# Attention products of two heads in turn on row and column tiles of TensorE, each chain held back until its banks and operands are there

## The chip, the cores and the metric

The kernel runs on one core of a Trainium2 chip. The metric is the device time of one execution in microseconds (us), as the median of the executions shown.

## What is computed

A decaying linear attention over 4 batches, 8 heads of 48 columns and 768 steps feeds a dense layer with a gated unit (384 to 2048 to 384), and that feeds a layer of eight experts, of which each token takes one (384 to 1024 to 384). All data are float32.

```python
f = 1.0 / (1.0 + np.exp(-f_logit))
for t in range(S):
    state = f[:, :, t, :, None] * state + np.einsum('bhd,bhe->bhde', k[:, :, t], v[:, :, t])
    y[:, :, t] = np.einsum('bhd,bhde->bhe', q[:, :, t], state)
...
h = x @ w_in
relu6 = np.clip(h + 3.0, 0.0, 6.0)
g = h * relu6 / 6.0
return (g @ w_out).astype(np.float32)
...
h = np.maximum(x[mask] @ w1[e], 0.0)
ye = h @ w2[e]
out[mask] = gate_w[mask, None] * eom[mask, e, None] * ye
```

## The kernel before

The 3072 tokens are worked in eight blocks (0 to 7) of 384 (TB): each batch is two blocks, its first half and its second. A block's attention is four **units** (pr 0 to 3), each for a pair of heads; there are 32 units, and the text numbers them n = 4 * block + pr. `attention` (from L199) does one unit. In SBUF the first head of a pair lies on partitions 0 to 47, the second on 64 to 111 (R is 112). A block has three chunks (c) of 128 tokens.

In a unit VectorE and ScalarE turn the decay into running products (two scans, L224 and L226) and scale keys and queries with them (kb L231, qt L233). Then TensorE works, all in plain float32:

- pk (L239): three transposes of the keys; ScalarE copies them to kn (L241).
- pa (L246): for each chunk and head a product of 48 rows by 128 columns, into one PSUM bank for each head; VectorE masks each bank into at (L248).
- pkv (L255, L256): keys by values, for the first head on columns 0 to 63 of the array and for the second from 64 on; VectorE adds them up into the running state st (L263 to L270), and ScalarE puts its negative into sbd (L274), one of two buffers in turn.
- py (L281, L282, L284): the unit's result. The values lie in DRAM with 96 columns, in which the two heads' columns alternate in groups of 16 and the other head's are zero. So three products of 96 columns on the whole array, one with the masked scores of each head and one with the state of both, add up to a chunk (two in the first chunk of a batch).

The result is split into a high and a low float32r part: xth by ScalarE (L290), xtl by VectorE (L291). Units 0 to 2 of a block fill 96 partitions each of one third of the block's 384 columns. The fourth fills the last 32 partitions of all three thirds, with three copies and three subtractions.

`mlp` (L301) then does the block's dense layer with products in three terms (high by high, high by low, low by high): 144 "up" products into ph (L296 to L298) and 144 "down" products into acc (L309 to L311), each 128 by 128 by 384. `between` issues the units of the next block among those of the current one, so that they are there when the next block begins. `choose` and `route` (px, pl, pt, pr) pick each token's expert and scatter its row to DRAM. After block 7 come the eight experts (yacc).

PSUM has three buffers for pk, pa, pkv, py, px, pl, pt and pr together (pool ps_m, tag m). The order on each engine isn't that of the code: a scheduler sets it at build time from a model of the engines' times (schedule_with_timeline_sim, last line), within the data's dependencies. On the chip each engine works its list in that order and waits at an instruction whose operands aren't there. All loads go through SP's queue in its own list's order. Weights of the dense layer are loaded and split on VectorE during the attention of blocks 0 and 1 (split64, L128 to L146); `fill` (L470) writes 16 blocks of padding to DRAM once the last of them is issued.

Of the kernel before, what the change touches and what calls it, by code (L numbers as in the profile page):

```python
# [10 lines left out]
F32 = mybir.dt.float32  # L11
F32R = mybir.dt.float32r
# [5 lines left out]
ALU = mybir.AluOpType  # L18
# [4 lines left out]
P = 128  # L23
B, H, S, D = 4, 8, 768, 48
NT = B * S
DM = H * D
KD = DM // P
FF = 2048
NF = FF // P
# [3 lines left out]
TB = 384  # L33
# [15 lines left out]
def fused(ctx: ExitStack, tc: tile.TileContext, q, k, fl, v, vt, w_in, w_out, wg, w1, w2, out):  # L49
# [123 lines left out]
    def raw_of_block(tag):  # L173
        return blkp.tile([P, KD, TB], F32R, tag=tag, name="raw").rearrange("p k t -> p (k t)").bitcast(F32)[:, 0:SW]

# [14 lines left out]


# [5 lines left out]
    for i in range(2):  # L197
        t = at1.tile([R, NCH, 96], F32, name=f"sbd{i}")
        nc.gpsimd.memset(t, 0.0)  # L199
        sbds.append(t)  # L200
    state, ready = {}, []

    def attention(blk, pr, xth, xtl):
# [6 lines left out]
        vs = at2.tile([P, NCH, 2, 96], F32, tag="vs", name="vs")  # L210
# [30 lines left out]
        nc.scalar.copy(kn, pk)  # L241
        at = at2.tile([P, 2, NCH, CH], F32, tag="at", name="at")
        pas = [ps_m.tile([P, NCH, CH], F32, tag="m", name=f"pa{x}") for x in range(2)]
        for c in range(NCH):
            for pa, rows in zip(pas, heads):
                nc.tensor.matmul(pa[:, c, :], lhsT=kb[rows, c, :], rhs=qt[rows, c, :], start=True, stop=True)  # L246
        for x, pa in enumerate(pas):
            nc.vector.tensor_tensor(out=at[:, x], in0=pa, in1=nmask[:, None, :].to_broadcast([P, NCH, CH]),  # L248
                                    op=ALU.mult)
# [3 lines left out]
        cols = lambda t, x: t.rearrange("p (j x i) -> p j x i", j=3, x=2)[:, :, x, :]  # L253
# [18 lines left out]
        for hf in range(2):  # L272
            rows = slice(64 * hf, 64 * hf + D)
            nc.scalar.mul(  # L274
                sbd[rows].rearrange("p c (j x i) -> p c j x i", j=3, x=2)[:, c0:, :, hf, :],
                st[rows, c0:, :].rearrange("p c (j i) -> p c j i", j=3), -1.0)
# [8 lines left out]
        if pr < 3:  # L285
            parts = [(slice(0, 96), slice(0, 96), pr)]
        else:
            parts = [(slice(96, 128), slice(32 * j, 32 * j + 32), j) for j in range(3)]
        for dst, src, j in parts:
            nc.scalar.copy(xth[dst, j, :], py[src])  # L290
            nc.vector.tensor_tensor(out=xtl[dst, j, :], in0=py[src], in1=xth[dst, j, :].bitcast(F32),  # L291
                                    op=ALU.subtract)
# [139 lines left out]
    SYNC = mybir.DependencyInfo(mybir.DependencyClass.Sync, mybir.DependencyReason.DATA)  # L432

# [3 lines left out]

    def after_all(ins, others):
        for o in others:
            tc.add_manual_dep(ins.ins, o.ins.name, SYNC, reason="scattered rows")  # L440

# [3 lines left out]
    def att_unit(blk, pr):  # L445
        if pr == 0:
            xts[blk] = [blkp.tile([P, KD, TB], F32R, tag=n, name=n) for n in ("xth", "xtl")]
        attention(blk, pr, *xts[blk])
# [145 lines left out]
    for blk in range(NB):  # L594
        if blk == NB - 1:
            attc.close()
            ma = second.enter_context(tc.tile_pool(name="ma", bufs=1, side="right", reuse_waits="tile"))
            rank()

            spare = cycle([partial(raw_of, work)] * 2 + [partial(raw_of_block, n) for n in ("xth", "xtl")])  # L600
# [18 lines left out]
        acc = mlp(blkp, *xts.pop(blk), *wfirst, NF, relu6, between)  # L619
# [56 lines left out]
    with tc.If(general > 0):  # L676
# [4 lines left out]
        with ExitStack() as es:  # L681
# [3 lines left out]
            zsel = gp.tile([R, 176], F32, name="zsel")  # L685
            nc.vector.memset(zsel, 0.0)
            nc.vector.memset(zsel[0:D, 80:81], 1.0)
            nc.vector.memset(zsel[64:R, 96:97], 1.0)
# [3 lines left out]
            with tc.For_i(0, B * H // 2, 1) as n:  # L692
# [6 lines left out]
                for e in range(D):  # L699
# [9 lines left out]
                    j, i = divmod(e, 16)  # L709
                    c = 80 - (32 * j + i)  # L710
# [8 lines left out]
        with ExitStack() as es:  # L719
# [5 lines left out]
            with tc.For_i(0, NB, 1) as nb:  # L725
# [4 lines left out]
                for pr in range(3):  # L730
                    nc.sync.dma_start(out=xg[0:96, pr, :],
                                      in_=yv[bass.ds(nb, 1), pr].rearrange("a p t -> p (a t)"))
                    nc.sync.dma_start(out=xg[96:P, pr, :],
                                      in_=yv[bass.ds(nb, 1), 3, 32 * pr:32 * pr + 32].rearrange("a p t -> p (a t)"))
# [48 lines left out]
def layouts(inp):  # L783
# [9 lines left out]
    v = np.asarray(inp["v"]).reshape(B * H // 2, 2, 2, NCH, CH, 3, 16).transpose(0, 2, 4, 3, 1, 5, 6)  # L793
    vp = np.zeros((B * H // 2, 2, CH, NCH, 2, 3, 2, 16), v.dtype)
    for x in range(2):
        vp[:, :, :, :, x, :, x] = v[:, :, :, :, x]
    v = vp.reshape(B * H // 2, 2, CH, NCH, 2, 96)
    vt = np.asarray(inp["v"]).reshape(B * H // 2, 2, S, D).transpose(0, 3, 1, 2)
    order = []
    for j in range(KD):  # L800
        for h0, js in ((2 * j, range(3)), (6, [j])):
            for i3 in js:
                for h in (h0, h0 + 1):
                    order += [h * D + 16 * i3 + i for i in range(16)]
# [29 lines left out]
```

## Time and profile before

| what | value |
|---|---|
| median of 3 runs | 886.04 us (884.87 to 886.79) |
| time of the profiled execution | 883.24 us |
| its span in the profile | 881.4 us |
| TensorE (PE) busy | 848.4 us, 96% of the span |
| VectorE (DVE) busy | 540.1 us, 61% |
| ScalarE (ACT) busy | 406.1 us, 46% |
| mean granted clock of TensorE | 0.972 |

A clock of 1.0 is 2.4 GHz, 0.5 is 1.2 GHz. A float32 product stands in the records as two matmuls, a float32r product as one. Starts are exact, ends of matmuls are modelled and overlap the next start; so the time that a product takes is read here from one start to the next.

### The profile page before, as it was taken

What the parts mean: (1) busy time and instruction counts of PE and PEld (TensorE: products, weight loads), DVE (VectorE), ACT (ScalarE), POOL (GpSimd) and SP (SyncE); (2) the same over time, 40 slices, a digit from 0 to 9 for tenths busy, and PEclk for the clock granted to TensorE, in tenths of its full rate; (3) what the DMA queues carried; (4) which work ended last, traced back from release to release, by engine and by line L of the source; (5) the groups of instructions that cost most, each with busy time, mean ns of one, the idle gap of its engine ahead of it and who ended that gap; (6) DMA issues with size and microseconds to landing.
All of it is one profiled execution on the core that took longest, in us unless ns stands there. A gap on an engine that the chain in (4) does not pass through costs nothing.

```text
span 881.4 us, 14159 instructions
## 1 busy us (share of the span) xinstructions
PE 848.4 (96%) x5370; PEld 788.6 (89%) x5370; DVE 540.1 (61%) x1138; ACT 406.1 (46%) x864; POOL 60.2 (7%) x103
## 2 busy tenths in 40 slices
PE   8589999999999999999999999999999999999994
PEld 4469999999999999999999998999898999999994
DVE  7999995678546579554668743446364453555441
ACT  4557574456335346533545533435354343454421
POOL 1000000100100100010010010010100011101111
PEclk8668999999999999999999999999999999999998
DMA  7554576222111022121122000014154064255510
GB/s 220 183 175 118 178 246 193 65 69 67 36 59 59 22 81 69 30 73 44 38 66 67 30 28 15 1 31 157 46 197 159 29 203 146 82 172 197 164 55 28
DMA packets 40106, 85.78 MB, mean 97 GB/s; under 512 B 5185, under 2 KB 23394, under 8 KB 40028
## 3 DMA queue, kind: packets, MB, share of 16 engines
q1 hardware_dynamic: 36748, 75.29, 27.3%
q0 software_dynamic: 3280, 9.49, 3.0%
q8 instruction: 44, 0.72, 0.3%
q14 instruction: 34, 0.28, 0.1%
HBM read 68.92 MB, written 16.26 MB: 97 GB/s over the span
## 4 chain that ended last, share of the span: by engine, by line
PE 67%; DMA 3%; DVE 2%; issue 1%; ACT 1%; SPq 0%; POOL 0%; POOLq 0%; DVEq 0%; ACTq 0%
PE ph L296 9%; PE ph L297 9%; PE ph L298 9%; PE acc L309 6%; PE acc L310 5%; PE acc L311 5%; PE yacc L297 4%; PE pa L246 4%; PE yacc L298 3%; PE yacc L296 3%; DMA raw<-in_w 2%; PE py L281 2%; PE py L284 1%; PE py L282 1%; PE py L583 1%
## 5 line engine op out<-in xcount | busy, mean ns | idle before, releaser
L297 PE MATMUL ph<-xtl,wih 128*128 128x384 f32 x384 | 132.1, 344 | 1.3 <-DVE xtl L291 1.3
L296 PE MATMUL ph<-xth,wih 128*128 128x384 f32 x384 | 131.5, 344 | 1.4 <-DVE gf L334 0.8
L309 PE MATMUL acc<-woh,gh 128*128 128x384 f32 x384 | 131.6, 344 | 0.4 <-ACT gh L335 0.4
L298 PE MATMUL ph<-xth,wil 128*128 128x384 f32 x384 | 131.6, 343 | 0.0
L310 PE MATMUL acc<-wol,gh 128*128 128x384 f32 x384 | 130.0, 339 | 0.0
L334 DVE SCALAR_TENSOR_TENSOR gf<-gf,ph 128x384 f32<-128x384 f32 x128 | 70.5, 552 | 96.4 <-ACT gf L333 95.7
L311 PE MATMUL acc<-woh,gl 128*128 128x384 f32 x384 | 124.2, 340 | 0.0
L333 ACT ACTIVATE gf<-ph,three 128x384 f32<-128x384 f32 x128 | 74.2, 581 | 102.0 <-PE ph L298 100.4
L340 DVE SCALAR_TENSOR_TENSOR hl<-ph,hh 128x256 fp32r<-128x256 f32 (+7 forms) x72 | 39.0, 543 | 88.9 <-ACT hh L339 81.4
L335 ACT CAST gh<-gf 128x384 fp32r<-128x384 f32 x128 | 65.4, 512 | 58.2 <-DVE gf L334 54.9
L339 ACT ACTIVATE hh<-ph 128x256 fp32r<-128x256 f32 (+7 forms) x72 | 34.5, 481 | 116.1 <-PE ph L298 110.9
L336 DVE TENSOR_TENSOR gl<-gf,gh 128x384 fp32r<-128x384 f32 x128 | 70.8, 554 | 27.6 <-ACT gh L335 26.9
L297 PEld LDWEIGHTS ph<-xtl,wih 128*128 128x128 f32 x384 | 73.1, 190 | 3.2 <-DVE xtl L291 2.2
L296 PEld LDWEIGHTS ph<-xth,wih 128*128 128x128 f32 x384 | 72.6, 190 | 3.3 <-DVE gf L334 1.4
L297 PE MATMUL yacc<-hl,w2h 128*128 128x256 f32 (+7 forms) x216 | 71.7, 338 | 2.5 <-DVE hl L340 2.5
L298 PEld LDWEIGHTS ph<-xth,wil 128*128 128x128 f32 x384 | 73.1, 190 | 1.2
L309 PEld LDWEIGHTS acc<-woh,gh 128*128 128x128 f32 x384 | 72.1, 188 | 1.7 <-ACT gh L335 0.7
L310 PEld LDWEIGHTS acc<-wol,gh 128*128 128x128 f32 x384 | 72.2, 188 | 1.0
L311 PEld LDWEIGHTS acc<-woh,gl 128*128 128x128 f32 x384 | 71.3, 188 | 0.8 <-DVE gl L336 0.2
L296 PE MATMUL ph<-xh,w1h 128*128 128x256 f32 (+7 forms) x216 | 71.9, 334 | 0.0
L297 PE MATMUL ph<-xl,w1h 128*128 128x256 f32 (+7 forms) x216 | 71.7, 332 | 0.0
L298 PE MATMUL ph<-xh,w1l 128*128 128x256 f32 (+7 forms) x216 | 71.5, 332 | 0.0
(159 smaller groups left out, 1593.7 us busy)
## 6 DMA issues: line engine op xcount, KB each, us to landing
raw<-in_w SPq DMA_DIRECT2D x24, 512.0 KB, 6.1
raw<-in_w SPq DMA_DIRECT2D x32, 384.0 KB, 3.6
vs<-in_v SPq DMA_DIRECT2D x32, 288.0 KB, 3.1
raw<-in_w_in SPq DMA_DIRECT2D x12, 512.0 KB, 3.9
raw<-in_w_out SPq DMA_DIRECT2D x12, 512.0 KB, 3.7
xt<-in_fl SPq DMA_DIRECT2D x32, 168.0 KB, 2.9
kt<-in_k SPq DMA_DIRECT2D x32, 168.0 KB, 2.3
qt<-in_q SPq DMA_DIRECT2D x32, 168.0 KB, 3.4
```

The source lines that it names most:

```text
L246: nc.tensor.matmul(pa[:, c, :], lhsT=kb[rows, c, :], rhs=qt[rows, c, :], start=True, stop=True)
L296: nc.tensor.matmul(ps, lhsT=wh, rhs=xh, start=first, stop=False)
L297: nc.tensor.matmul(ps, lhsT=wh, rhs=xl, start=False, stop=False)
L298: nc.tensor.matmul(ps, lhsT=wl, rhs=xh, start=False, stop=last)
L309: nc.tensor.matmul(acc[t], lhsT=gh[:, ts_], rhs=w2h[:, f, :], start=f == 0, stop=False)
L310: nc.tensor.matmul(acc[t], lhsT=gh[:, ts_], rhs=w2l[:, f, :], start=False, stop=False)
L311: nc.tensor.matmul(acc[t], lhsT=gl[:, ts_], rhs=w2h[:, f, :], start=False, stop=f == nf - 1)
L333: nc.scalar.activation(gf, ph, AF.Relu, bias=three)
L334: nc.vector.scalar_tensor_tensor(out=gf, in0=gf, scalar=6.0, in1=ph, op0=ALU.min, op1=ALU.mult)
L335: nc.scalar.copy(gh, gf)
L336: nc.vector.tensor_tensor(out=gl, in0=gf, in1=gh.bitcast(F32), op=ALU.subtract)
L340: nc.vector.scalar_tensor_tensor(out=gl, in0=ph, scalar=0.0, in1=gh.bitcast(F32), op0=ALU.max, op1=ALU.subtract).ins)
```

## The change

- pa: the products of the two heads are issued in turn (second head, first head, then the next chunk), in an order that the scheduler has to keep (`in_turn`).
- py: the values and the state of each head get 64 columns of their own (48 and 16 of zeros). Each chunk is two products for each head, one with the scores and one with the state, on 64 columns of the array: the first head's on columns 0 to 63, the second's on 64 to 127, in turn.
- pkv: the same products as before, in turn, second head first.
- The first pa product of a unit waits for kn and for the subtraction that freed the unit before's py bank (`after_all(products[0], freed)`); the first py product waits for both masks and both state copies (`after_all(products[0], masked)`).
- xth and xtl become one tile xx. A unit's copy and subtraction cover 128 partitions. The fourth unit of a block goes to a tile yx instead, and six transfers from SBUF to SBUF carry its rows to their places in xx. Rows of w_in are reordered on the host to match.
- The branch for extreme decays and loads, which these inputs don't take, follows the new layout.

```diff
@@ -238,22 +247,24 @@
         kn = at1.tile([P, NCH, R], F32, tag="kn", name="kn")
-        nc.scalar.copy(kn, pk)
+        freed[0:1] = [nc.scalar.copy(kn, pk)]
         at = at2.tile([P, 2, NCH, CH], F32, tag="at", name="at")
         pas = [ps_m.tile([P, NCH, CH], F32, tag="m", name=f"pa{x}") for x in range(2)]
-        for c in range(NCH):
-            for pa, rows in zip(pas, heads):
-                nc.tensor.matmul(pa[:, c, :], lhsT=kb[rows, c, :], rhs=qt[rows, c, :], start=True, stop=True)
+        products = [nc.tensor.matmul(pas[x][:, c, :], lhsT=kb[heads[x], c, :], rhs=qt[heads[x], c, :], start=True,
+                                     stop=True) for c in range(NCH) for x in (1, 0)]
+
+        after_all(products[0], freed)
+        in_turn(products)
+        masked = []
...
-        for c in range(NCH - half):
-            nc.tensor.matmul(pkv[0:64, c, :], lhsT=kn[:, c, 0:64], rhs=cols(vs[:, c, 0, :], 0), start=True, stop=True)
-            nc.tensor.matmul(pkv[64:R, c, :], lhsT=kn[:, c, 64:R], rhs=cols(vs[:, c, 1, :], 1), start=True, stop=True)
+        wide = (slice(0, 64), heads[1])
+        in_turn([nc.tensor.matmul(pkv[wide[x], c, :], lhsT=kn[:, c, wide[x]], rhs=vs[:, c, x, 0:D], start=True,
+                                  stop=True) for c in range(NCH - half) for x in (1, 0)])
...
-        py = ps_m.tile([96, TB], F32, tag="m", name="py")
+        for x in range(2):
+            masked.append(nc.scalar.mul(sbd[heads[x], c0:, x, 0:D], st[heads[x], c0:, :], -1.0))
+        py = ps_m.tile([P, TB], F32, tag="m", name="py")
+        products = []
         for c in range(NCH):
             cs = slice(c * CH, (c + 1) * CH)
             first = half == 0 and c == 0
-            nc.tensor.matmul(py[:, cs], lhsT=vs[:, c, 0, :], rhs=at[:, 0, c, :], start=True, stop=False)
-            nc.tensor.matmul(py[:, cs], lhsT=vs[:, c, 1, :], rhs=at[:, 1, c, :], start=False, stop=first)
+            halves = [(x, py[64 * x:64 * x + 64, cs]) for x in (1, 0)]
+            products += [nc.tensor.matmul(o, lhsT=vs[:, c, x, :], rhs=at[:, x, c, :], start=True, stop=first)
+                         for x, o in halves]
             if not first:
-                nc.tensor.matmul(py[:, cs], lhsT=sbd[:, c, :], rhs=qt[:, c, :], start=False, stop=True)
...
+                products += [nc.tensor.matmul(o, lhsT=sbd[:, c, x, :], rhs=qt[:, c, :], start=False, stop=True)
+                             for x, o in halves]
+        after_all(products[0], masked)
+        in_turn(products)
+
+        yx = xx[:, :, pr, :] if pr < 3 else at1.tile([P, 2, TB], F32R, tag="yx", name="yx")
+        nc.scalar.copy(yx[:, 0, :], py)
+        freed[1:] = [nc.vector.tensor_tensor(out=yx[:, 1, :], in0=py, in1=yx[:, 0, :].bitcast(F32), op=ALU.subtract)]
+        if pr == 3:
+            for j in range(KD):
+                for x in range(2):
+                    nc.sync.dma_start(out=xx.bitcast(F32)[64 * x + D:64 * x + 64, :, j, :],
+                                      in_=yx.bitcast(F32)[64 * x + 16 * j:64 * x + 16 * j + 16])
```

TensorE's list, first half of unit 18 (block 4), before: pa_3512 is the bank of the first head, pa_3513 that of the second.

```order
L239 MATMUL pk<-ident,kb 128x112 x2
L246 MATMUL pa_3512<-qt,kb 128x128 [waits DMAHW1_49,PE_49]
L246 MATMUL pa_3512<-qt,kb 128x128 x2
L310 MATMUL acc_3103<-wol,gh 128x384
...
L297 MATMUL ph<-xtl,wih 128x384
L246 MATMUL pa_3513<-qt,kb 128x128 [waits DVE_49]
L246 MATMUL pa_3513<-qt,kb 128x128 x2
L298 MATMUL ph<-xth,wil 128x384
...
L255 MATMUL pkv<-vs,kn 64x48 [waits DMAHW3_49,Activation_49]
```

The same place with the change:

```order
L253 MATMUL pa_3566<-qt,kb 128x128 [waits DMAHW0_49,DVE_49,Activation_49]
L253 MATMUL pa_3565<-qt,kb 128x128 [waits PE_49]
L253 MATMUL pa_3566<-qt,kb 128x128
L253 MATMUL pa_3565<-qt,kb 128x128
...
L266 MATMUL pkv<-vs,kn 48x48 [waits DMAHW4_49,PE_49]
...
L291 MATMUL py<-at,vs 64x128 [waits DVE_49,Activation_49]
L291 MATMUL py<-at,vs 64x128 x3
L294 MATMUL py<-qt,sbd_160 64x128 x2
```

Before, the two heads' pa chains stand apart, with seven products of the dense layer between them, and pkv stands five further on. Now the six pa products are one chain with the heads in turn, pkv follows at once, and 28 products of the dense layer stand between pkv and py, which is one chain too.

TensorE's list at the entrance of block 3, before: the end of unit 15's py (sbd_160), then what follows it up to the block's first up product.

```order
L284 MATMUL py<-qt,sbd_160 96x128
L246 MATMUL pa_2853<-qt,kb 128x128 [waits Activation_49]
...
L297 MATMUL ph<-xtl,wih 128x384
...
L281 MATMUL py<-at,vs 96x128 [waits DVE_49]
...
L310 MATMUL acc_2333<-wol,gh 128x384
...
L296 MATMUL ph<-xth,wih 128x384
```

The same place with the change, unit 15's py and unit 16's pa and pkv, up to block 3's first up product:

```order
L294 MATMUL py<-qt,sbd_160 64x128 x2
L248 MATMUL pk<-ident,kb 128x112 [waits PE_49]
L248 MATMUL pk<-ident,kb 128x112 x2
L253 MATMUL pa_2900<-qt,kb 128x128 [waits DMAHW2_49,DVE_49,Activation_49]
L253 MATMUL pa_2899<-qt,kb 128x128 [waits PE_49]
...
L266 MATMUL pkv<-vs,kn 48x48 [waits DMAHW4_49]
...
L310 MATMUL ph<-xx,wih 128x384 [waits DMAHW1_49,DMAHW0_49]
```

Before, 38 products of the dense layer (24 and 14) stand between unit 15's py and block 3's first up product. Now none does, and that product waits for two of the six transfers.

SP's list with the change, ahead of the six transfers of unit 7 (for block 1); the two xs_d rows are the last of the 16 fills:

```order
L479 DMA xs_d<-pad 128x3x388 [waits DMAHW0_49]
L481 DMA xs_d<-pad 128x388 [waits DMAHW1_49]
L223 DMA vs<-in_v 128x384 [waits DMAHW2_49,PE_49]
L221 DMA qt<-in_q 112x384 [waits DMAHW3_49,PE_49]
L305 DMA xx<-yx 16x2x384 [waits DMAHW4_49,DVE_49]
L305 DMA xx<-yx 16x2x384 [waits DMAHW5_49]
```

Before, block 1's tiles needed no transfer; now its six stand behind the fills.

## Rows read from the trace of the kernel before

**Rows 1.** Busy times by stretch: stretch, us, then each engine's busy us, PEclk, DMA, GB/s.

```profile
63.33:71.60 8.27, 7.44 (x24) 6.27 (x25) 8.24 (x17) 5.99 (x14) 0.00 (x0) 0.50 0.34 105
71.60:140.00 68.40, 68.40 (x453) 65.15 (x453) 64.41 (x129) 43.42 (x92) 0.00 (x0) 1.00 0.67 212
140.00:553.00 413.00, 412.51 (x2770) 386.39 (x2769) 254.80 (x586) 192.17 (x442) 20.48 (x30) 1.00 0.17 52
```

**Rows 2.** Waits of TensorE from 72 to 553 us: total, times, longest.

```profile
PE py L284 <- ACT sbd L274: 0.5, 1, 0.5
```

**Rows 3.** Groups on TensorE from 140 to 553 us: matmul records and busy us.

```profile
L246 PE MATMUL pa<-qt,kb 48*128 48x128 f32 x276 | 41.8, 291 | 0.0
```

**Rows 4.** Timeline of TensorE, one head's pa chain in unit 18: start, us, what.

```profile
472.57 0.33 PE L296 MATMUL ph<-xth,wih 128*128 128x384 f32 x1
472.75 0.34 PE L297 MATMUL ph<-xtl,wih 128*128 128x384 f32 x1
473.01 0.93 PE L246 MATMUL pa<-qt,kb 48*128 48x128 f32 x6
473.88 0.44 PE L298 MATMUL ph<-xth,wil 128*128 128x384 f32 x1
474.16 0.34 PE L296 MATMUL ph<-xth,wih 128*128 128x384 f32 x1
```

**Rows 5.** The same view, py products of unit 17.

```profile
467.10 0.38 PE L281 MATMUL py<-at,vs 128*96 128x128 f32 x2
467.32 0.38 PE L282 MATMUL py<-at,vs 128*96 128x128 f32 x2
```

**Rows 6.** The same view, unit 0, where both heads' pa stand together.

```profile
9.15 0.94 PE L246 MATMUL pa<-qt,kb 48*128 48x128 f32 x12
10.02 0.91 PE L69 MATMUL warm<-kb,pad 112*128 112x384 f32 x2
```

**Rows 7.** The same view, pkv of unit 17 (12 records from 462.61 on), and what follows.

```profile
462.61 0.26 PE L255 MATMUL pkv<-vs,kn 128*64 128x48 f32 x1
...
463.09 0.46 PE L281 MATMUL py<-at,vs 128*96 128x128 f32 x2
```

**Rows 8.** Copies and masks behind the chains: least, median and most ns.

```profile
L290 ACT CAST xth<-py x48: 457/472/493, 16.9 to 555.7; 96x384 fp32r<-96x384 f32 x24, 32x384 fp32r<-32x384 f32 x24
L291 DVE TENSOR_TENSOR xtl<-py,xth x48: 528/552/557, 17.3 to 556.3; 96x384 fp32r<-96x384 f32 x24, 32x384 fp32r<-32x384 f32 x24
L248 DVE TENSOR_TENSOR at<-pa,nmask x64: 528/557/559, 10.4 to 545.6; 128x384 f32<-128x384 f32 x64
```

**Rows 9.** SP's issues, back to back, and kt's time from issue to landing (last number, us).

```profile
0.81 0.41 SPq L212 DMA_DIRECT2D xt<-in_fl  x1
1.28 0.41 SPq L212 DMA_DIRECT2D kt<-in_k  x1
kt<-in_k SPq DMA_DIRECT2D x32, 168.0 KB, 2.3
```

**Rows 10.** SP's issues of the 16 fills, first and last, and their landing.

```profile
121.23 0.43 SPq L471 DMA_DIRECT2D xs_d<-pad  x1
...
136.96 0.88 SPq L473 DMA_DIRECT2D xs_d<-pad  x1
xs_d<-pad SPq DMA_DIRECT2D x8, 582.0 KB, 6.9
```

**Rows 11.** TensorE's clock early on: a long wait in the timeline, and stretches.

```profile
42.89 0.82 PE L239 MATMUL pk<-ident,kb 112*128 112x112 f32 x3 [3.32 <-DVE kb L231]
37.50:40.90 3.40, 1.34 (x9) 0.90 (x8) 3.33 (x9) 2.43 (x7) 0.00 (x0) 1.00 0.67 215
40.90:51.20 10.30, 8.31 (x42) 5.98 (x43) 10.09 (x23) 4.85 (x11) 0.00 (x0) 0.50 0.56 178
69.46 0.52 PE L297 MATMUL ph<-xtl,wih 128*128 128x384 f32 x1
69.78 0.52 PE L298 MATMUL ph<-xth,wil 128*128 128x384 f32 x1
```

More of the change, by code (lines that the diff above doesn't have):

```diff
@@ L189, in load_second, with after_all @@
         return [partial(first, kt) for kt in range(KD)] + [partial(second, i) for i in range(NFE // 2)]
+    SYNC = mybir.DependencyInfo(mybir.DependencyClass.Sync, mybir.DependencyReason.DATA)
+    def after_all(ins, others):
+        for o in others:
+            tc.add_manual_dep(ins.ins, o.ins.name, SYNC, reason="all of them first")
     zero = at1.tile([R, TB], F32, name="zero")
@@ L197, in fused, with in_turn, attention @@
     for i in range(2):
-        t = at1.tile([R, NCH, 96], F32, name=f"sbd{i}")
+        t = at1.tile([R, NCH, 2, 64], F32, name=f"sbd{i}")
         nc.gpsimd.memset(t, 0.0)
         sbds.append(t)
-    state, ready = {}, []
-    def attention(blk, pr, xth, xtl):
+    state, ready, freed = {}, [], []
+    ORDER = mybir.DependencyInfo(mybir.DependencyClass.NoSync, mybir.DependencyReason.DATA)
+    def in_turn(products):
+        for a, b in zip(products, products[1:]):
+            tc.add_manual_dep(b.ins, a.ins.name, ORDER, reason="one head after the other")
+    def attention(blk, pr, xx):
         b, half = divmod(blk, 2)
@@ L271, in attention @@
         c0 = 1 - half
[L272 to L276, printed above, removed]
-        py = ps_m.tile([96, TB], F32, tag="m", name="py")
+        for x in range(2):
+            masked.append(nc.scalar.mul(sbd[heads[x], c0:, x, 0:D], st[heads[x], c0:, :], -1.0))
+        py = ps_m.tile([P, TB], F32, tag="m", name="py")
+        products = []
         for c in range(NCH):
@@ L280, in attention @@
             first = half == 0 and c == 0
-            nc.tensor.matmul(py[:, cs], lhsT=vs[:, c, 0, :], rhs=at[:, 0, c, :], start=True, stop=False)
-            nc.tensor.matmul(py[:, cs], lhsT=vs[:, c, 1, :], rhs=at[:, 1, c, :], start=False, stop=first)
+            halves = [(x, py[64 * x:64 * x + 64, cs]) for x in (1, 0)]
+            products += [nc.tensor.matmul(o, lhsT=vs[:, c, x, :], rhs=at[:, x, c, :], start=True, stop=first)
+                         for x, o in halves]
             if not first:
-                nc.tensor.matmul(py[:, cs], lhsT=sbd[:, c, :], rhs=qt[:, c, :], start=False, stop=True)
[L285 to L292, printed above, removed]
+                products += [nc.tensor.matmul(o, lhsT=sbd[:, c, x, :], rhs=qt[:, c, :], start=False, stop=True)
[10 more added lines that the diff above has]
+                                      in_=yx.bitcast(F32)[64 * x + 16 * j:64 * x + 16 * j + 16])
     def mm3(ps, wh, wl, xh, xl, first, last):
@@ L436, in free_of @@
             tc.declare_no_dep(ins.ins, o.ins, reason="rows of their own")
-    def after_all(ins, others):
-        for o in others:
-            tc.add_manual_dep(ins.ins, o.ins.name, SYNC, reason="scattered rows")
     xts = {}
@@ L446, in att_unit @@
         if pr == 0:
-            xts[blk] = [blkp.tile([P, KD, TB], F32R, tag=n, name=n) for n in ("xth", "xtl")]
-        attention(blk, pr, *xts[blk])
+            xts[blk] = blkp.tile([P, 2, KD, TB], F32R, tag="xx", name="xx")
+        attention(blk, pr, xts[blk])
     wfirst = first_weights(m1)
@@ L598, in fused @@
             rank()
-            spare = cycle([partial(raw_of, work)] * 2 + [partial(raw_of_block, n) for n in ("xth", "xtl")])
+            two = blkp.tile([P, 2, KD, TB], F32R, tag="xx", name="xx").rearrange("p h k t -> p h (k t)").bitcast(F32)
+            spare = cycle([partial(raw_of, work)] * 2 + [lambda: two[:, 0, 0:SW], lambda: two[:, 1, 0:SW]])
             for part in weights(0, ma, lambda: next(spare)()):
@@ L618, in fused @@
         between(-1)
-        acc = mlp(blkp, *xts.pop(blk), *wfirst, NF, relu6, between)
+        xx = xts.pop(blk)
+        acc = mlp(blkp, xx[:, 0], xx[:, 1], *wfirst, NF, relu6, between)
         if blk == NB - 1:
@@ L708, in fused @@
                     nc.vector.tensor_tensor(out=sg, in0=sg, in1=qg, op=ALU.mult)
-                    j, i = divmod(e, 16)
-                    c = 80 - (32 * j + i)
+                    c = D - 1 - e
                     for t in range(2):
@@ L729, in fused @@
                 yv = ya_d.rearrange("h (b r) p t -> (h b) r p t", r=4)
[L730 to L734, printed above, removed]
+                for j in range(KD):
+                    for x in range(2):
+                        for dst, pr, src in ((64 * x, j, D * x), (64 * x + D, 3, D * x + 16 * j)):
+                            n = D if pr < 3 else 16
+                            nc.sync.dma_start(out=xg[dst:dst + n, j, :],
+                                              in_=yv[bass.ds(nb, 1), pr, src:src + n].rearrange("a p t -> p (a t)"))
                 split(xth, xtl, xg, nc.gpsimd)
@@ L790, in pairs @@
         return np.ascontiguousarray(o.reshape(B * H // 2, P, S)[:, :R])
[L793 to L797, printed above, removed]
+    v = np.asarray(inp["v"]).reshape(B * H // 2, 2, 2, NCH, CH, D).transpose(0, 2, 4, 3, 1, 5)
+    v = np.concatenate([v, np.zeros(v.shape[:-1] + (64 - D,), v.dtype)], -1)
     vt = np.asarray(inp["v"]).reshape(B * H // 2, 2, S, D).transpose(0, 3, 1, 2)
@@ L800, in layouts @@
     for j in range(KD):
[L801 to L804, printed above, removed]
+        for x in range(2):
+            order += [(2 * j + x) * D + i for i in range(D)] + [(6 + x) * D + 16 * j + i for i in range(16)]
     w_in = np.asarray(inp["moe_w_in"])[np.array(order)].reshape(KD, P, FF).transpose(1, 0, 2)
```

16 lines of the change are left out of this document (6 added, 10 removed).

## The prediction

> **What bounds the kernel now.** First the busy times by stretch [rows 1]. From 140 to 553 us TensorE is busy 412.51 of 413.00 us, at full clock, and VectorE 254.80. The list of waits for 72 to 553 us holds one wait of 0.5 us [rows 2]. So there TensorE's own list is the time, and each us taken from it is a us gained, as long as nothing else makes it wait. From 71.60 to 140 VectorE is nearly full as well (64.41 of 68.40), because it splits the dense layer's weights; before that TensorE waits for it and runs at half clock (0.50 from 63.33 to 71.60). After 553 us no attention is left. The group of pa has 276 records from 140 to 553, 12 to a unit, so 23 of the 32 units lie in the stretch where TensorE alone counts [rows 3].
>
> **pa.** Read the timeline by starts. An up product takes 0.18 us (472.57 to 472.75). At a chain of three pa products of one head the step into it is 0.26, the chain 0.87 (473.01 to 473.88), the first product behind it 0.28 [rows 4]. Against 0.17 to 0.18 for a usual step that is 0.09 + 0.87 + 0.11 = 1.07 us for a chain. In unit 0 both heads' products stood in turn already, at full clock: 12 records from 9.15 to 10.02, 0.87 us, as long as one head's alone [rows 6]. So the second head is free when the two alternate, and a unit saves one chain, 1.07 us.
>
> **py.** A product takes 0.22 us (467.10 to 467.32) [rows 5]. A unit has 9 in a second half and 8 in a first (no state in the first chunk), 8.5 on average: 1.87 us. Now there are 12 or 10, in pairs. The trace has no pair of column tiles with 128 moving columns, so I bound it. If a pair takes as long as one product: 5.5 by 0.22, 1.21 us. If the two don't overlap at all: 11 by 0.22, 2.42. The nearest row is pkv, which has just this form, two column tiles on all rows, with 48 moving columns: 12 records from 462.61 to 463.09, 0.48 us with the change of tiling at its end [rows 7]. One py record of 128 columns takes 0.11 us, so one of 48 should take at least 48/128 of it, 0.041, and 12 in a row 0.50 before any such change is added (0.09 to 0.11 at pa). They did overlap. I take the full pair. py also gains a step into its tiling and out of it: 0.09 + 0.11, and 0.10 for its first weights, which nothing hides, as at pa. Net: 1.87 - 1.21 - 0.30 = 0.36 us saved.
>
> The Trainium skill ("TensorE: Matmul & The Clock Gate", Part 3, the measured speedups) gives 2.38 for three column tiles instead of 3. By the same share two tiles would give 1.59, an estimate by that page: the sum would come out some 8 us later. No run here has shown it.
>
> **pkv** has the same products. In 14 of the 23 units it stood alone before; now it follows pa, which saves a step in and out (0.20): 0.12 us on average. A unit saves 1.07 + 0.36 + 0.12 = 1.55 us, and 23 units **35.7 us** (29 to 39: half of py's gain lost, or py's steps in and out free).
>
> **Before 140 us** some 3.5 units run beside the dense layer, which would be 5.4 us. But VectorE is nearly full there, and block 0 starts later: before, its first up products ran between the fourth unit's three subtractions; now they wait for yx's subtraction, which stands later in VectorE's list, and for the transfers. Against that the last split of weights stands 20 operations earlier in that list, some 10 us at 0.50 each (64.41 us for 129). I take **3 us** gained (7 gained to 4 lost).
>
> **Copies.** A copy takes 0.47 us and a subtraction 0.55 whether it covers 96 or 32 partitions [rows 8], so 128 should cost no more, and the fourth unit's three of each become one. Off TensorE's path this is worth nothing. The values are also a third fewer bytes; loads are hidden in this stretch (DMA share 0.17 [rows 1]).
>
> **The six transfers.** Behind the fourth unit's py now come a copy (0.47), a subtraction (0.55), six issues at 0.47 us each on SP (0.81 to 1.28) and a landing, which I take as kt's 2.3 us [rows 8, 9]. The first up products need the first two transfers: some 4.1 us after py. At the entrances of blocks 2, 4 and 6 the list has 25 to 29 dense products, pk, pa and pkv in between, about 6 us: hidden. At the others it isn't:
> - Blocks 3 and 5: py is followed by pk (0.33), then pa, which now waits for the subtraction: start at about 1.3, so 0.9 us lost. pa and pkv end at 2.6; the up product waits until about 4.1. Together **2.4 us each**.
> - Block 7: nine dense products, then px, which waits for copies of acc, and pl, which waits for copies of px (0.47 each as for xth, in a row on ScalarE): about **1.2 us**.
> - Block 1: its transfers stand behind the 16 fills on SP, which took from 121.23 to 136.96 to issue, and a fill 6.9 us to land [rows 10]. Weights end earlier, so the fills do too; py of unit 7 stands 45 dense products and a unit ahead of the entrance, some 10 us. **3 us** (0 to 6).
>
> Together 9 us (5 to 14).
>
> **The clock.** After the wait of 3.32 us that ended at 42.89 the clock was at half from 40.90 to 51.20, and a dense product took 0.32 instead of 0.17 us (69.46 to 69.78) [rows 11]. Since 71.6 no wait has been as long, and none has cost the clock. Waits of 2.4 to 3 us at three entrances may. The wait at 42.89 was followed by thin work, these by dense products, so I let half clock last a third of that stretch, 3.4 us: a product takes 0.32 for 0.17, so 0.47 of it is lost, 1.6 us for each fall; if it lasts 10.3 as there, 5. I take **4 us** (0 to 15).
>
> **Waits inside units.** py now waits for both masks and both state copies at once; before, the scheduler put its products in one by one. 23 to 34 dense products (4.0 to 5.9 us) cover two masks of 0.56 [rows 8], the state sums and the copies. I take **2 us** (0 to 5).
>
> **Sum.** -35.7 - 3 + 9 + 4 + 2 = -23.7 us, on the profiled execution's 883.24: 859.5. The median of the runs is 2.8 us above that execution, so the forecast is 862 us; with the terms' ends 851 to 872.
>
> **Rivals.**
> - *The clock falls at every odd entrance and stays low as long as in rows 11.* For it: waits near 3 us, which no stretch since 71.6 has had. Against it: dense work follows at once, which it didn't at 42.89. Three falls of 5 us and a longer block 1: 13 us more, 875.
> - *Each chain's wait shows in every unit.* The first product of a chain now needs everything; VectorE works its own list in order, and a mask behind a scan comes late. 1 us in each of 23 units: 885. Against it: the cover of 4 us and more, and VectorE's 62% there.
> - *The two heads' py products don't overlap*, and the change ends slower. Their row strips are the same, all 128; only the columns differ. Then a pair takes 0.44 us, 1.21 more in each of 26.5 units: 32 us, 894. The sum turns to a loss once a pair takes 0.39 us (24 us over 26.5 by 5.5 pairs is 0.165 more than 0.22). Against it: pkv [rows 7], though its margin is small. The Trainium skill speaks for it (the same page, Part 3, "What overlaps and what doesn't": weights load beside a running product only where the row groups differ); by that rule, the trace disagrees for pkv and has nothing on py.
>
> **Chances.** Forecast 0.66, clock 0.20, waits 0.05, no overlap 0.09. The range runs from 849 (TensorE's saving at its upper end and no fall of the clock) to 880, which takes in the clock rival and leaves the other two out. A measurement of this kernel can tell about 0.2%, 1.8 us, from no change. Faster: the forecast and most of the clock rival, 0.84; same, mainly the waits rival, 0.05; slower 0.11.
>
> **What would show it.** In the new profile a unit's pa is one chain of 12 records in some 0.87 us, py's 24 or 20 records take about 1.3 or 1.1 us, and the wait list from 140 to 553 us has waits of pa for the subtraction and of up products for yx transfers at blocks 1, 3 and 5, 2 to 3 us each, and little else. I am wrong if py's chains take 2 us or more, if PEclk falls below 1 for long in that stretch, or if pa and py have waits in most units.

## The result, and the profile after

The changed kernel takes 870.38 us (median of 4 runs, 869.02 to 871.37) beside 885.45 for the kernel before on the same chip: a ratio of 0.9833 [0.9805, 0.9861]. The forecast was 862, with a range of 849 to 880. Measured again beside the experiments it took 868.86, ratio 0.9798 [0.9766, 0.983]. Its profiled execution has a span of 868.6 us, the one of before 881.4.

Busy times by stretch of the changed kernel, the view of [rows 1]:

```profile
25.70:70.10 44.40, 27.50 (x161) 20.53 (x162) 42.31 (x85) 25.36 (x57) 0.00 (x0) 0.50 0.61 175
140.00:553.00 413.00, 401.95 (x2985) 374.00 (x2986) 254.14 (x590) 193.70 (x445) 21.41 (x30) 0.99 0.17 50
411.50:414.90 3.40, 1.84 (x26) 1.65 (x27) 2.22 (x8) 0.56 (x2) 0.00 (x0) 0.99 0.54 143
414.90:418.30 3.40, 3.40 (x13) 2.96 (x12) 2.83 (x5) 1.97 (x5) 0.00 (x0) 0.50 0.30 54
```

From 140 to 553 us TensorE was idle for 0.49 us before and is idle for 11.05 now. Its waits from 137 to 605 us, where [rows 2] had a single one:

```profile
PE ph L310 <- DMA xx<-yx: 5.6, 4, 2.4
PE py L291 <- ACT sbd L284: 2.7, 3, 1.2
PE ph L310 <- DVE gf L348: 2.5, 4, 0.8
PE pa L253 <- ACT kn L250: 1.6, 2, 0.8
PE pa L253 <- ACT th L230: 0.8, 1, 0.8
PE acc L323 <- ACT gh L349: 0.7, 1, 0.7
PE pl L374 <- ACT xTh L367: 0.6, 1, 0.6
```

Half of that stands at block entrances. At block 5 it reads like this in the timeline of TensorE, and in those of VectorE and SP (last two lines):

```profile
409.39 0.39 PE L291 MATMUL py<-at,vs 128*64 128x128 f32 x4
409.61 0.39 PE L294 MATMUL py<-qt,sbd 112*64 112x128 f32 x4
...
410.37 0.51 PE L248 MATMUL pk<-ident,kb 112*128 112x112 f32 x3
411.66 0.94 PE L253 MATMUL pa<-qt,kb 48*128 48x128 f32 x12 [0.78 <-ACT kn L250]
412.53 0.56 PE L266 MATMUL pkv<-vs,kn 128*48 128x48 f32 x12
414.49 0.41 PE L310 MATMUL ph<-xx,wih 128*128 128x384 f32 x1 [1.41 <-DMA xx<-yx]
...
411.00 0.56 DVE L301 TENSOR_TENSOR yx<-py,yx 128x384 fp32r<-128x384 f32 x1 [4.72 <-ACT yx L300]
...
411.58 3.77 SPq L305 DMA_DIRECT2D xx<-yx  x6
```

Read three things in it. A pair of py products (four records, two to a product) starts 0.22 us after the one before it, as long as one product took in [rows 5]: the second head is free. Both heads' pa are one chain of 12 records in 0.87 us. And behind the fourth unit's py TensorE waits 0.78 us at pa and 1.41 us for the transfers; 3.4 us at half clock follow (last row of the first fence). The view puts the wait at pa down to kn, but kn's copy ends at 411.41 us and the unit's subtraction on VectorE at 411.56; pa starts at 411.66, so the subtraction came last.

To see where the time went I compare equal work, with the first px of block 0's choose and of block 7's as marks (142.69 and 619.55 us before, 137.08 and 605.45 after), and add up the time from each product's start to the next one's:

| between the marks | before: records, us | after |
|---|---|---|
| pa | 276, 38.5 | 276, 20.0 |
| py | 392, 42.3 | 508, 31.4 |
| pkv, with waits behind it | 228, 9.6 | 228, 12.7 |
| px, with waits behind it | 63, 5.6 | 63, 12.9 |
| up and down products | 1980, 362.0 | 2016, 372.4 |
| all | 476.9 | 468.4 |

Where TensorE waits, the wait counts with the product before it. Of the dense products 36 have moved behind the first mark, 6.2 us at 0.1735 each. At equal work the stretch up to the first mark is 0.6 us longer, the middle 14.7 shorter, the end 1.3 longer: 12.8 us, the difference of the spans. In the middle the waits are 14.5 us (the list above) for 1.4, and 20 dense products at half clock take 3.0 us more than at full. Without these the products fell by 14.7 + 13.1 + 3.0 = 30.8 us, 1.34 a unit.

### The profile page after: what moved, and what is told of

Same layout as the page of the kernel before. It is cut to its first block, busy times and chain, and to the rows that moved or that the text cites. A ratio compares the mean times of both kernels' runs of the same rounds, so it can differ in the third digit from the quotient of the medians.

```text
span 868.6 us, 14585 instructions
## 1 busy us (share of the span) xinstructions
PE 808.3 (93%) x5530; PEld 748.6 (86%) x5530; DVE 528.4 (61%) x1122; ACT 398.1 (46%) x848; POOL 61.1 (7%) x103
## 4 chain that ended last, share of the span: by engine, by line
PE 46%; DVE 5%; DMA 4%; ACT 2%; issue 2%; SPq 0%; POOL 0%; POOLq 0%; DVEq 0%; ACTq 0%
PE ph L310 7%; PE ph L312 7%; PE ph L311 7%; PE yacc L311 4%; PE yacc L312 3%; PE acc L323 3%; PE acc L324 3%; PE acc L325 3%; PE yacc L310 3%; DMA raw<-in_w 3%; PE py L591 1%; PE py L291 1%; PE pa L253 1%; PE px L553 1%; DVE w1l L124 1%
## 5 line engine op out<-in xcount | busy, mean ns | idle before, releaser
L310 PE MATMUL ph<-xx,wih 128*128 128x384 f32 x384 | 133.7, 348 | 9.5 <-DMA xx<-yx 6.3
L312 PE MATMUL ph<-xx,wil 128*128 128x384 f32 x384 | 132.9, 346 | 0.0
L311 PE MATMUL ph<-xx,wih 128*128 128x384 f32 x384 | 131.9, 343 | 0.0
L323 PE MATMUL acc<-woh,gh 128*128 128x384 f32 x384 | 129.4, 337 | 0.7 <-ACT gh L349 0.7
L325 PE MATMUL acc<-woh,gl 128*128 128x384 f32 x384 | 122.0, 337 | 0.0
L310 PEld LDWEIGHTS ph<-xx,wih 128*128 128x128 f32 x384 | 74.0, 193 | 13.0 <-DMA xx<-yx 7.2
L312 PEld LDWEIGHTS ph<-xx,wil 128*128 128x128 f32 x384 | 73.9, 192 | 0.9 <-issue 0.5
L311 PEld LDWEIGHTS ph<-xx,wih 128*128 128x128 f32 x384 | 73.9, 192 | 0.3
```

The lines of the kernel that those rows point to most:

```text
L310: nc.tensor.matmul(ps, lhsT=wh, rhs=xh, start=first, stop=False)
L311: nc.tensor.matmul(ps, lhsT=wh, rhs=xl, start=False, stop=False)
L312: nc.tensor.matmul(ps, lhsT=wl, rhs=xh, start=False, stop=last)
L323: nc.tensor.matmul(acc[t], lhsT=gh[:, ts_], rhs=w2h[:, f, :], start=f == 0, stop=False)
L325: nc.tensor.matmul(acc[t], lhsT=gl[:, ts_], rhs=w2h[:, f, :], start=False, stop=f == nf - 1)
```

## The experiments

My theory when they began: each part is worth what its own products save, and the waits at the entrances are the landing of the transfers. The rival: the waits belong to the rule that a chain's first product waits for the whole chain.

**One part alone: pa** (in the kernel before).

```
+        products = [nc.tensor.matmul(pas[x][:, c, :], lhsT=kb[heads[x], c, :], rhs=qt[heads[x], c, :], ...
+                    for c in range(NCH) for x in (1, 0)]
+        after_all(products[0], freed)
+        in_turn(products)
```

> The kernel before with one part of the change: a unit's six pa products in turn, the first of them after the copy kn and the subtractions that free the bank. py keeps its 96 columns, there are no yx transfers and the values keep their layout. Theory (each part is worth what its own products save, and the waits at block entrances belong to the transfers): pa fell by 18.5 us between the two compared places, pkv behind it by 2 to 3, and nothing is paid back, so 885.5 - 20 = 865 us (862 to 869), faster than the whole change. Rival (the waits belong to the first product's wait for the whole chain, whichever chain it is): half of the 14.5 us of waits comes with it, 872 us or more.

Measured: 881.32 us, ratio 0.9947 [0.9924, 0.997]. The theory missed; the rival's "872 us or more" holds, but by more than the half of the waits that it counted on. pa did fall, from 38.5 to 22.1 us in the middle, but at equal work the middle is only 3.8 us shorter than before. Most of the rest was lost at the entrances of blocks 2, 4 and 6. There TensorE (first four rows) waits piece by piece for the three subtractions of the fourth unit, which stand in VectorE's list (the rows behind) between the scans of the next units:

```profile
344.36 0.59 PE L311 MATMUL ph<-xth,wih 128*128 128x384 f32 x2
345.85 0.44 PE L312 MATMUL ph<-xtl,wih 128*128 128x384 f32 x1 [0.90 <-DVE xtl L306]
347.51 0.62 PE L311 MATMUL ph<-xth,wih 128*128 128x384 f32 x2 [0.70 <-ACT xth L305]
349.76 0.44 PE L312 MATMUL ph<-xtl,wih 128*128 128x384 f32 x1 [1.63 <-DVE xtl L306]
...
345.25 0.55 DVE L306 TENSOR_TENSOR xtl<-py,xth 32x384 fp32r<-32x384 f32 x1
345.83 0.96 DVE L236 TENSOR_TENSOR_SCAN gg<-th,zero 112x384 f32<-112x384 f32 x1
...
348.17 0.95 DVE L238 TENSOR_TENSOR_SCAN r<-xt,rmax 112x384 f32<-112x384 f32 x1
349.15 0.55 DVE L306 TENSOR_TENSOR xtl<-py,xth 32x384 fp32r<-32x384 f32 x1
...
351.67 0.56 DVE L306 TENSOR_TENSOR xtl<-py,xth 32x384 fp32r<-32x384 f32 x1
```

From the first subtraction to the last it is 6.4 us. The clock then stood at half for 23.9 us in the middle, 6.8 to 10.2 at each of the three entrances:

```profile
350.90:357.80 6.90, 5.68 (x35) 5.15 (x34) 6.05 (x13) 3.25 (x8) 0.00 (x0) 0.51 0.19 50
```

**The other part: py and the transfers**, with pa's products as before.

```
-        products = [nc.tensor.matmul(pas[x]...) for c in range(NCH) for x in (1, 0)]
-        after_all(products[0], freed)
-        in_turn(products)
+        for c in range(NCH):
+            for pa, rows in zip(pas, heads):
+                nc.tensor.matmul(pa[:, c, :], lhsT=kb[rows, c, :], rhs=qt[rows, c, :], start=True, stop=True)
```

> The whole change without its pa part: pa's products stand as before, no wait of the first for the copy and the subtraction. py in pairs with its wait, the yx transfers and pkv in turn stay. Theory (parts add up): 870.4 + 18.5 for pa and 2 for pkv, which no longer follows pa: 889 to 892 us, slower than before, since py's 10.9 us are less than the 14.5 us of waits and 3 us of low clock that come with it. Rival (the waits at the entrances come from pa's wait for the subtraction in front of them): they go, and it is 875 to 882 us.

Measured: 883.38 us, 0.9962 [0.9941, 0.9984], nearer to the rival, though above its range. The transfers are there, and TensorE hardly waits for them (146 to 617 us; the rows left out are 0.4 us and less):

```profile
PE pl L372 <- ACT xTh L365: 1.4, 2, 0.7
PE ph L308 <- DMA xx<-yx: 0.5, 1, 0.5
...
```

The clock is full from 75.2 to 870.5 us. What differs is the list: at block 3 eleven down products now stand between the fourth unit's py and the entrance, where the whole change has none. py fell to 31.4 us as in the whole change; at equal work the middle is 7.1 us shorter than before, the stretch ahead of it 5 us longer. So the transfers alone aren't the wait: they become one where no dense products stand between py and the entrance.

**No first wait.**

```
-        after_all(products[0], freed)
-        after_all(products[0], masked)
```

> The whole change, but no chain's first product waits for more than its own operands and bank; the order within a chain stays. Theory: TensorE now takes one product early and the rest later, so two chains per unit are split and step into and out of their tiling once more, 2 x 0.2 x 23 = 9 us; the transfers are late at the entrances as before; of the 22 us of waits of py for sbd in the early blocks at most 5 come back: 872 to 879 us, slower than the change. Rival (the first product's wait makes most of the 14.5 us of waits): 857 to 863 us.

Measured: 877.41 us, 0.9908 [0.9882, 0.9935], inside the theory's range, for other reasons than it gave. The chains are torn, and that costs more than 9 us: pa takes 28.9 instead of 20.0 in the middle, py 39.1 instead of 31.4. But the waits there fall from 14.5 us to 3.1. So the waits come with the first wait, and the whole chain that it keeps is worth more than they cost. That it acts through the place in the list that it gives a chain is my reading; no run keeps the list and drops the wait.

**The transferred unit first.**

```
-        attention(blk, pr, xts[blk])
+        attention(blk, (pr + 3) % 4, xts[blk])
```

Here the copies of the three later units cover all 128 rows, and so leave zeros where the fourth unit's rows should be; the products are as many as in the change.

> The whole change, with a block's units computed in the order fourth, first, second, third: the unit whose rows are moved by the six transfers comes first, three units ahead of the entrance, and the last one writes its rows in place. The work is the same. Theory (the waits of the up products are the landing of the transfers): the 5.6 us of waits for transfers between 137 and 605 us go, and the two falls of the clock behind entrances (3 us) with them: 861 us (858 to 865). Rival (the entrance waits for whatever comes last, and the third unit's copy and subtraction take the place of the transfers): 867 to 871 us.

Measured: 876.79 us, 0.9897 [0.9855, 0.9939]: slower than the change; the theory and the rival both missed. No wait for a transfer is left between 140 and 615 us, but 14.3 us of waits for gf, six of them, the longest at even entrances, and the clock stood at half for 23.9 us there. TensorE's up products now come earlier in the list; their activation stands behind the masks and scans in VectorE's:

```profile
347.43 0.40 PE L312 MATMUL ph<-xx,wil 128*128 128x384 f32 x1
351.91 0.69 PE L310 MATMUL ph<-xx,wih 128*128 128x384 f32 x1 [4.08 <-DVE gf L348]
...
348.10 1.01 DVE L260 TENSOR_TENSOR at<-pa,nmask 128x384 f32<-128x384 f32 x2
...
349.14 0.95 DVE L233 TENSOR_TENSOR_SCAN gg<-th,zero 112x384 f32<-112x384 f32 x1
...
351.32 0.99 DVE L348 SCALAR_TENSOR_TENSOR gf<-gf,ph 128x384 f32<-128x384 f32 x2
```

So a new theory: an entrance costs what is late there less the dense products that the list leaves to cover it. The next kernels leave all work as it is and move some of that cover.

**The change again, as the control.**

> The changed kernel once more, on the same chip as the runs beside it: 870 us (868 to 873) by every theory.

Measured: 868.86 us (867.16 to 869.57). Its clock fell at blocks 1 and 3, not at 1 and 5.

**Down products behind the fourth unit's py.** A block's last 18, or its last 9, are kept back until that py (of the next block) has run:

```
+        if pr == 3:
+            tail[blk] = products[-1]
...
-                nc.tensor.matmul(acc[t], lhsT=gh[:, ts_], rhs=w2h[:, f, :], start=f == 0, stop=False)
+                o = nc.tensor.matmul(acc[t], lhsT=gh[:, ts_], rhs=w2h[:, f, :], start=f == 0, stop=False)
+                if f == nf - LAG and nxt in tail:
+                    in_turn([tail[nxt], o])
```

With 18 products, as here:

> The whole change, and the last 18 down products of a block (those of its last two hidden tiles) placed behind the py of the next block's fourth unit, so that at the entrances of blocks 3, 5 and 7 they run while the transfers land. Theory (the waits there are the landing of the transfers and the bank behind them): 1.0 + 1.6 + 1.0 us at each of blocks 3 and 5 and one fall of the clock go, about 9 us; py now has fewer products ahead of it and waits 1 to 2 us for its masks and state at three entrances: net 4 to 6 us, 865 us (862 to 868). Rival (TensorE is short of work there and the wait only moves to py): 869 to 873 us.

With 9 (`f == nf - 1`):

> The same with only the last 9 down products behind that py. Theory: 9 products are 1.6 us, and with pk, pa and pkv some 3.4 us stand against the 4.1 of copy, subtraction, issue and landing, so 0.7 us of wait stays at blocks 3 and 5, and py has cover enough: 865 us (862 to 868). Rival: 869 to 873 us.

Measured with 18: 875.21 us, 0.9872 [0.984, 0.9904], above both ranges; with 9: **865.23 us**, 0.9756 [0.9721, 0.9791], as the theory had it, and each of its runs below each of the control's (862.61 to 867.08 against 867.16 to 869.57). Eighteen are too many: py then waits for its state copies (6.0 us, 4 times), and at blocks 4 and 6 the up products wait some 2 us for the transfers behind pk (the longest 2.1), with 6.8 us at half clock behind each. With nine, the transfers' waits are short, and the clock is full all through the middle (two rows of waits from 137 to 599 us, then the stretch):

```profile
PE ph L313 <- DMA xx<-yx: 3.1, 6, 0.8
...
PE py L292 <- ACT sbd L285: 1.6, 2, 1.0
...
137.40:598.80 461.40, 450.81 (x3288) 420.39 (x3286) 283.70 (x660) 220.13 (x494) 26.61 (x36) 1.00 0.18 54
```

The middle is 461.5 us here for 468.4 in the change, with the same products between the marks.

**py by head, not in turn.**

```
+        for x in (1, 0):
+            for c in range(NCH):
```

> The whole change, but py's products stand first all of one head, then all of the other, instead of in turn; all else is the same. Theory (the second head is free because it stands on the other column tile right behind the first): without the turn nothing overlaps, 508 products of some 0.11 us take 55 us for 31.4 in the stretch that was compared, and the earlier units lose as well: 893 us (888 to 898), slower than before. Rival (a product of 64 columns on its own costs half of one of 96 or more, so that the order does not matter): 868 to 873 us.

Measured: 885.36 us, 0.9998 [0.9975, 1.0022]: the whole gain is gone, though the time stays below the theory's range. py takes 50.3 us for 31.4, where the theory had 55. The timeline shows why not more:

```profile
418.32 0.38 PE L291 MATMUL py<-at,vs 128*64 128x128 f32 x2
418.55 0.38 PE L293 MATMUL py<-qt,sbd 112*64 112x128 f32 x2
418.76 0.44 PE L291 MATMUL py<-at,vs 128*64 128x128 f32 x4
418.99 0.44 PE L293 MATMUL py<-qt,sbd 112*64 112x128 f32 x4
```

A product of one head alone takes 0.22 us (two records). Only in the middle, where one head's last chunk and the other's first meet, two pairs run together (four records in 0.22). So this unit takes ten times 0.22 us where six pairs would do. The theory, with nothing overlapping, had missed those two. It had also left the waits and the clock as they were: they came to 10.1 us for 14.5 (140 to 619 us), and the clock stayed full. The turn is what makes the column tiles pay.

**The change without column pairs, the new layout and transfers**: pa in turn as in e1, and py's 8 or 9 old products kept together too.

```
+        masked.append(...)
+        after_all(products[0], masked)
+        in_turn(products)
```

> The kernel before with pa in turn as in e1, and py's products kept together too, the first of them behind both masks and both state copies; py keeps its 96 columns (8 or 9 products), no yx transfers. So it is the change without column pairs and transfers. Theory (what e1 lost, it lost at block entrances, where the up products were placed right behind the last unit's py and waited for its copy and subtraction, with the clock at half behind it): here the up products stand one pk behind that py at every second entrance, so the waits are there again: 872 to 880 us. Rival (e1 lost because py was torn apart at the entrances): 863 to 868 us, the whole of pa's saving.

The same with nine down products behind that py:

> The same with the last 9 down products of a block behind the py of the next block's fourth unit, as in e5b. Theory: 1.6 us of dense work covers the copy (0.47) and the subtraction (0.55) where these aren't held up by VectorE's list: pa's 18 us remain and the entrances cost 3 us or less: 867 us (864 to 871). Rival (VectorE's list holds the subtraction longer than nine products last): 873 to 880 us.

Measured: 903.87 us, 1.019 [1.0159, 1.0221], and 901.88, 1.0174 [1.014, 1.0207]: both slower than before, which no theory had. From 148 to 638 us the first of them waits 18.7 us, most of it for the three pieces of the fourth unit and for gf behind VectorE's list, and stands at half clock for 37.5:

```profile
PE ph L317 <- DVE xtl L311: 7.0, 6, 2.0
PE ph L316 <- DVE gf L354: 5.4, 5, 1.3
PE ph L316 <- ACT xth L310: 3.0, 5, 0.9
PE pa L256 <- issue: 2.5, 3, 1.1
PE py L298 <- ACT sbd L289: 0.8, 1, 0.8
```

Nine down products don't cover that. At equal work the first of them is 8.6 us longer than before up to the first mark, 10.3 in the middle and 3.2 behind it, so the middle holds about half of its loss; what made the early part longer stays open. Between this and the change lie 35 us, of which py's products are 45.9 - 31.4 = 14.5, some of them at half clock.

**The early part.** e5b without the first waits in block 0, and then also the fills earlier.

```
-        after_all(products[0], freed)
+        if blk > 0:
+            after_all(products[0], freed)
...
-        after_all(products[0], masked)
+        if blk > 0:
+            after_all(products[0], masked)
```

> e5b, but in block 0 no chain's first product waits for the whole chain (the order in a chain stays). Theory (until the first routing VectorE, ScalarE and the loads set the end, and TensorE's waits there only move): the first px of block 0's routing comes within 1.5 us of where it was, 863 to 867 us. Rival (the 22 us in which py's first product waits for the state copies, most of them before 75 us, are time lost): 850 to 860 us.

```
-            if blk == 0 and f >= NF - E:
+            if blk == 0 and 2 <= f < 2 + E:
                 with tc.issue_after(loads[-1].ins):
-                    fill(f - NF + E)
+                    fill(f - 2)
```

> e9, with the 16 fills issued from the third to the tenth hidden tile of block 0 on, between the loads of the weights, instead of in its last eight. Theory (block 1's up products wait because its transfers stand behind the fills on SP and their bytes): the wait of 2.6 us at that entrance goes, and the fall of the clock behind it (3.4 us at half, 1.6 lost): 858 us (855 to 861). Rival (the fills then hold up the loads of the weights, and the dense layer of block 0 waits instead): 862 to 868 us.

Measured: **862.0 us**, 0.9734 [0.9708, 0.9759], the fastest of all, a us below the theory's range and above the rival's; its interval lies below the control's and overlaps e5b's. The first px comes at 136.29 us, 1.1 earlier than in e5b. The changed kernel's largest early wait (first row) has shrunk to the third row here, and one for the transfers of block 0 has come in its place (second row); the last row stood in the changed kernel too, with 5.0 us:

```profile
PE py L291 <- ACT sbd L284: 19.7, 5, 5.1
```

```profile
PE ph L315 <- DMA xx<-yx: 6.7, 1, 6.7
PE py L296 <- ACT sbd L286: 6.7, 4, 2.9
PE pk L249 <- DVE kb L241: 6.1, 3, 2.6
```

The waits move and the end of the part hardly does: some 20 us of py's waits for the state were worth about one. With the fills early it took 864.1 us, 0.9755 [0.9737, 0.9772], the rival's case. The wait for the transfers at block 1 went (none over 0.7 us is left behind 141 us), yet the first px comes 1.7 us later at equal work, with up products waiting 3.0 us for gf ahead of it (1.2 in e9) and 3.4 us at half clock.

## Why the prediction was right, and where it wasn't

**pa: right in kind, its step too large.** Twelve records in 0.87 us, as in unit 0 [rows 6]. In the middle pa's own row gave 18.5 us, 0.81 a unit, where the forecast had 0.87 for the chain and 0.20 for the steps ahead of it and behind it, which count in the rows of its neighbours. The 0.20 takes every chain to stand between dense products. Before, that was so for only part of them: of 47 pieces of pa in the middle 24 came behind a dense product and 30 went ahead of one, and the others shared a step with pk, pkv or py.

**py: right.** "If a pair takes as long as one product" was the end taken, and it holds: 0.22 us. py's own row gave 10.9 us, 0.47 a unit; the forecast's 0.36 also has the step into it, which that row leaves out. With that the rival "the two heads' py products don't overlap" fell, and so did the rule that spoke for it. The Trainium skill ("TensorE: Matmul & The Clock Gate", Part 3, "What overlaps and what doesn't") lets weights load beside a running product only where the row groups differ; here both products of a pair use the same rows, and the trace disagrees, 0.22 us for both.

**pkv: its steps went, but another came.** Without waits behind it pkv takes 9.8 us in the middle (e4), 9.6 before: the same products. The steps that it spares stand in its neighbours' rows. Before, in 14 units, a pkv by itself began 0.27 us after the dense product ahead of it, for 0.17 to 0.18 otherwise (unit 18):

```profile
474.68 0.34 PE L296 MATMUL ph<-xth,wih 128*128 128x384 f32 x1
474.95 0.26 PE L255 MATMUL pkv<-vs,kn 128*64 128x48 f32 x1
```

and the dense product behind pa took 0.28 [rows 4]. Now pkv begins 0.87 us after pa (411.66 to 412.53 us above), as long as a pa chain took up to a dense product before (473.01 to 473.88 in [rows 4]). So both steps, some 0.2 us, are gone in those 14 units, as forecast. But before, py stood right behind pkv in 19 of the 23 units [rows 7]; now a dense product does in each, and it takes 0.28 us too (343.08 to 343.36 at block 4). Some 0.1 us in 19 units leaves about 0.03 of the 0.12 a unit, an estimate from these steps.

Together the products gave 1.34 us a unit for the 1.55 forecast, 30.8 us for 35.7. How the rest of the missing 0.21 us splits over the steps into and out of the tilings stays open.

**Before 140 us: nothing gained, within its bounds.** -3 was taken; +0.6 came in this execution and -0.4 in the control's. VectorE, named as the bound, is busy for 62.30 of the first 72 us and 59.04 of the next 65; no run parts it from ScalarE and the loads. The half clock doesn't account for the difference: up to the first mark it lasted 51.2 us here (44.4 of them in the first row of the first fence), 41.0 in the control and 41.0 in e5b, which at equal work came 0.3 us later than this execution. e9 prices the first waits of block 0 at about a us.

**The six transfers: right.** Forecast 3 us at block 1 and 2.4 at blocks 3 and 5; measured 2.44 at block 1, and 0.78 + 1.41 at block 5, the two waits in the order that was told. That entrances 2, 4 and 6 are hidden was nearly right: there it is mostly the next unit's py that waits, for its state (2.7 us in all, for the 2 forecast as waits inside units). At block 4 pa also waits 0.80 us, for a subtraction that stands behind two scans on VectorE and ends 0.1 us before pa starts (341.74 and 341.84; the list of waits names th), and an up product 0.30 for the transfers. What the forecast lacked are short waits behind px: of the 7.3 us that px's row grew by, 2.4 are the wait at block 1, 1.7 waits of up products for gf at blocks 2, 3 and 5, and 0.6 pl's wait at block 7, where 1.2 had been forecast for px and pl; the other 2.5 stay open.

**The clock: right, 3.0 us for 4.** Two falls of 3.4 us, as long as had been assumed; that length was a third of a longer fall, taken without a row that showed it, so the match is luck. The rival, long falls at every odd entrance, didn't happen.

**Copies: wrong in a way that the time didn't show.** "Off TensorE's path this is worth nothing" was said of the fourth unit's three copies and subtractions that become one. e1 and e8 point to it as a part that the rest needs: with pa's chain kept whole and three pieces, the entrance waits for the third, and the clock falls for 6.8 to 13.7 us at a time. That it is the pieces is argued from these waits and not shown: no kernel had the new layout and the transfers with py's old products. The sum didn't need this because the change did all of it at once, and that is luck.

So the sum came out near, 859.5 forecast for the profiled execution (870.31), 11 us off: the products are 5 us short, the early part 4, the waits and the clock together (16.1 for 15) 1, the end 1. Its bounds were added up wrongly: the ends of the five terms give 845 and 895 us, not 851 and 872, and the two that are named for 849 give 855. The result lies inside all of them.

## What to carry to other kernels

Two products on column tiles cost one if they stand next to each other in the list. In this layout keeping a chain whole was worth more than the waits that it brings (e3); with the old layout at the entrances it was not (e8). A part's saving arrives only where the list leaves dense work against what is late at the next stage: price an edit with the place that the scheduler gives it, not alone. Here moving nine products, with no work changed, was worth another 0.4%.

## What I had not expected of the hardware

- Equal waits didn't have equal effects on the clock. Blocks 3 and 5 have the same two waits of 0.8 and 1.4 us; in one execution the clock fell to 0.50 at block 5 (414.90 to 418.30), in the control's at block 3 (275.70 to 279.10), and in e7 at neither. With waits of at most 1.0 us (e5b) it stayed at 1.00 from 137 to 599 us.
- Nor did the longer wait have the larger effect. In e5b, ahead of that stretch, one wait of 2.70 us left the clock at 1.00 (first two rows); in e10 two of 0.89 and 0.73 us were followed by 3.4 us at half.

```profile
123.05 0.45 PE L313 MATMUL ph<-xx,wih 128*128 128x384 f32 x1 [2.70 <-DVE gf L353]
123.20:126.60 3.40, 3.40 (x37) 2.98 (x37) 2.90 (x6) 2.52 (x7) 0.00 (x0) 1.00 1.06 359
...
110.37 0.79 PE L333 MATMUL acc<-woh,gl 128*128 128x384 f32 x3 [0.89 <-DVE gl L357]
111.89 0.52 PE L315 MATMUL ph<-xx,wih 128*128 128x384 f32 x1 [0.73 <-DVE gf L355]
112.10:115.50 3.40, 3.40 (x19) 2.96 (x20) 3.40 (x7) 2.63 (x6) 0.00 (x0) 0.50 0.55 119
```

- Two py products that stand on different column tiles run together even where each head's list is kept apart, for the two chunks that happen to be neighbours (four records in 0.22 us in e7).
